# Two sets of transposes issued sooner, and one ScalarE relu, in a kernel bound by TensorE

## The chip, the cores, the metric

The kernel runs on one core of one Trainium2 chip. The metric is the device time of one execution in microseconds (us); lower is better. All executions quoted here are of the fast state, with a granted TensorE clock between 0.997 and 1.000. The engines are called PE (TensorE; PEld is its weight loads), VectorE (DVE in the profile), ScalarE (ACT), POOL (GpSimd) and SP (SyncE).

## The reference, cut to what matters

```python
# q, k, v: (8 batches, 8 heads, 576 rows, 64); w_in: 512 x 2048; w_out: 2048 x 512
kv  = einsum('bhsd,bhse->bhde', k, v)          # linear attention: no softmax
out = einsum('bhsd,bhde->bhse', q, kv)
x   = out / sqrt(mean(out*out, -1) + 1e-6) * g_norm    # per head; then (4608, 512)
h   = x @ w_in
g   = where(h > 0, h, exp(min(h, 0)) - 1)              # elu
y   = g @ w_out
```

Almost all of the work is in the two products of the last lines.

## The kernel before

The kernel works in nine stages: 512 rows of each of the eight batches, numbered 0 to 7, and a ninth stage for the rows left over. Stage T's expansion (`mm1`: eight products `i` of 256 hidden columns, 8 matmuls of 128x512 each) is interleaved with the contraction of stage T-1 (`mm2`) and with the attention of stage T+1 (the k-v products, the scores `out`, their norm), whose small matmuls stand between the large ones. **The program order on each engine is fixed by the order of the code**; nothing is reordered by a scheduler.

PSUM is the memory that TensorE writes its results to. Its eight banks are shared out like this: `at` is one tile of two banks, `mm1` two tiles of two banks each, and `mm2` two tiles of one bank each. Where all products use the `mm1` tiles, as in batch 2, product `i+2` takes the banks of product `i`, and PE cannot start it before the last reader of product `i` is done.

```python
def mm1(T, i, ..., relu=False, home="m1", between=()):
    ...                                   # 8 matmuls into both = [128, 2, 512] fp32 PSUM
    return elu(T, i, parts, relu, between)

def elu(T, i, parts, relu, between=()):
    e = mlpt.tile([P, 2, G], BF16, name="elu_e", tag="elu_e")
    for lo, hi, ps in parts:
        nc.scalar.activation(e[:, lo:hi, :], ps, AF.Exp)          # reads PSUM
    ...
    if relu:
        h = mlpt.tile([P, 2, G], BF16, name="elu_h", tag="elu_h", bufs=2)
        for lo, hi, ps in parts:
            nc.scalar.activation(h[:, lo:hi, :], ps, AF.Relu)     # last reader of PSUM
        parts = [(0, 2, h)]
    def rest():
        for lo, hi, h in parts:
            nc.vector.tensor_scalar(out=e..., in0=e..., 1.0, 1.0, op0=ALU.min, op1=ALU.subtract)
            nc.vector.tensor_tensor(out=gT[T]..., in0=e..., in1=h,
                                    op=ALU.add if relu else ALU.max)  # without relu: h is PSUM
    return rest
```

With `relu`, elu(h) is min(exp(h),1)-1 + relu(h), and ScalarE's relu is the last to read the PSUM banks. Without it, elu(h) is max(min(exp(h),1)-1, h), and VectorE's maximum, later in the chain, is the last to read them.

The normalised rows `xs` are turned into xT by PE transposes in batches 1 and 2 (later batches use DMA transposes), followed by a multiplication with g on the way out of PSUM:

```python
def x_u(u, eng):                          # batch 1: u = 0 on ScalarE, 1 on VectorE
    def turn(ps):
        for n in range(2):
            c = 2 * u + n
            for j in range(J):
                nc.tensor.transpose(xt[:, n, ...], st["xs"][:, j, c * P : c * P + P], ident)
        ...                               # xT[:, 2u:2u+2] = xt * g
```

`x_t` does the same for batch 2. The places at which these are called:

```python
    for j in range(J):                    # stage 0's contraction, f = 10, 11
        mm2(0, j, 10, 12)
        if j == 1:
            at["inv1"]()
            at["xu0"](scores[:, 0, :])
    at["mulu1"]()                         # VectorE: second half of xs
    ...
    for j in range(J):
        mm2(0, j, 12, 14)
    for j in range(J):
        mm2(0, j, 14, FC, hold=j > 1)     # FC = 16: two matmuls for each j
        if j == 2:
            at["xu1"](scores[:, 1, :])
    mm2_out(0, 2); mm2_out(0, 3)
    # ... [cut] then stage 1: mm1(1, 0) to mm1(1, 7), scores, norms of batch 2
    at["x0"]()
    mm2_quarter(1, 2, 0)                  # = mm2(1, 2, 0, 4): four matmuls
    at["x1"](ps_m1.tile([P, 2, G], FP32, name="xt_ps", tag="mm1")[:, 0, :])
    mm2_quarter(1, 2, 1)
    # ... [cut] stages 2 to 8:
        group(T, at, lead, second, {2: (1, 2, 4), B: ()}.get(T, (4, 5)))   # last: which i get the relu
```

## Time and profile before

| | before |
|---|---|
| time, median of 3 runs | 284.67 us (284.57 to 284.71) |
| span of the profiled run | 283.0 us |
| PE busy | 277.2 us, 98% |
| VectorE busy, ScalarE busy | 159.7 us, 153.5 us |

The page of the kernel before. The lines of groups give: line, engine, operation, output and input, their shapes, count, then busy us and mean ns of one, then the engine's idle time before them and what ended it.

```profile
span 283.0 us, 5186 instructions
PE 277.2 (98%) x2146; PEld 129.4 (46%) x2146; DVE 159.7 (56%) x231; ACT 153.5 (54%) x221; POOL 54.4 (19%) x96
...
PE 95%; DMA 2%; DVE 1%; issue 0%; SPq 0%; ACT 0%; DVEq 0%
...
L496 DVE TENSOR_TENSOR gT<-elu_e,h_ps 128x1024 bf16<-128x1024 bf16 (+1 forms) x52 | 61.4, 1180 | 5.8 <-DVE elu_e L488 0.5
...
L483 ACT ACTIVATE elu_h<-h_ps 128x1024 bf16<-128x1024 f32 (+1 forms) x19 | 18.5, 988 | 0.0
L496 DVE TENSOR_TENSOR gT<-elu_e,elu_h 128x1024 bf16<-128x1024 bf16 x19 | 13.2, 693 | 2.8 <-ACT elu_h L483 1.5
```

PE is 98% busy and 95% of the chain of work that ended last, so only time in which PE issues nothing can be won. "98% busy" hides what is left of it, because a matmul's shown duration (379 ns) is longer than the distance at which matmuls follow each other (216 ns): a stall of up to 160 ns leaves no idle time in the page. **The place to look is the distance between starts.** The timeline shows it, with a merged run of n matmuls lasting (n-1) x 216 + 379 ns when nothing is lost: 1.89 us for eight.

The timeline of the kernel before, at the three places that matter (start us, duration us, engine, line, operation, count; in brackets the idle time ahead and what ended it):

```profile
45.52 0.61 PE L413 MATMUL se_ps<-ident,xs 128*128 128x128 bf16 x8
45.97 0.59 PE L512 MATMUL o_ps<-w_out_sb,gT 128*128 128x512 bf16 x2
46.24 0.75 DVE L422 TENSOR_SCALAR xT<-se_ps,g_col 128x1024 bf16<-128x1024 bf16 x1 [1.67 <-PE se_ps L413]
46.40 2.10 PE L465 MATMUL at<-xT,w_in_sb 128*128 128x512 bf16 x8
...
68.03 1.28 DVE L229 TENSOR_TENSOR xs<-se_ps,ss 128x512 bf16<-128x512 f32 x2
70.14 0.61 PE L305 MATMUL xt_ps<-ident,xs 128*128 128x128 bf16 x8
70.58 1.03 PE L512 MATMUL o_ps<-w_out_sb,gT 128*128 128x512 bf16 x4
70.78 0.75 DVE L314 TENSOR_SCALAR xT<-xt_ps,g_col 128x1024 bf16<-128x1024 bf16 x1 [1.48 <-PE xt_ps L305]
71.59 0.60 PE L465 MATMUL h_ps<-xT,w_in_sb 128*128 128x512 bf16 x2
...
87.41 1.02 ACT L477 ACTIVATE elu_e<-h_ps 128x1024 bf16<-128x1024 f32 x1
89.49 1.22 DVE L496 TENSOR_TENSOR gT<-elu_e,h_ps 128x1024 bf16<-128x1024 bf16 x1
89.71 1.03 PE L512 MATMUL o_ps<-w_out_sb,gT 128*128 128x512 bf16 x4
90.77 1.02 PE L465 MATMUL h_ps<-xT,w_in_sb 128*128 128x512 bf16 x4
```

Three losses can be read here. At 46.40, eight matmuls of batch 1's first product take 2.10 us instead of 1.89: inside that run the third matmul, the first to need xT's second half, starts at 47.05, 214 ns late, when VectorE's multiplication (to 47.00) is done. At 71.59, batch 2's first product should have followed the four `o_ps` matmuls at 70.58 + 4 x 0.216 = 71.44; it is 148 ns late, released by the multiplication that ended at 71.54. At 90.77, batch 2's product 7 should have come at 89.71 + 0.864 = 90.57; it is 192 ns late, released by VectorE's maximum of product 5, which read PSUM until 90.71. Together that is 0.55 us. (Starts were read instruction by instruction; the two digits of the lines give the same within 10 ns.)

### The profile page before, as it was taken

To read this page: it belongs to the slowest core of one execution; us is meant where nothing else is said; L and a number is where in the kernel's file an instruction comes from. 1 tells how busy PE (TensorE), PEld (TensorE's weight loads), DVE (VectorE), ACT (ScalarE), POOL (GpSimd) and SP (SyncE) were. 2 spreads that over 40 slices of the span, in tenths; PEclk is the share of its full clock that TensorE was granted. 3 is DMA by queue.
4 is the path that set the end of the run, shared out by engine and by line. 5 is a ranking of instruction groups with operands and counts; after the bars stand their busy time and mean duration, and the time that the engine had idled before them with its cause. 6 is when DMAs were issued, how large, how long until landed. Compare 5 with 4: busy or idle time off the path is not lost.

```text
span 283.0 us, 5186 instructions
## 1 busy us (share of the span) xinstructions
PE 277.2 (98%) x2146; PEld 129.4 (46%) x2146; DVE 159.7 (56%) x231; ACT 153.5 (54%) x221; POOL 54.4 (19%) x96
## 2 busy tenths in 40 slices
PE   8999999999999999999999999999999999999994
PEld 3444544445444444444444444444444444444443
DVE  2359343877488646943694468445854585444400
ACT  2779546666486438533763378237923692333311
POOL 7834422151421331005200421012000000000000
PEclk9999999999999999999999999999999999999999
DMA  7999999696993695358935794355233123010122
GB/s 193 204 204 202 207 200 185 213 149 121 199 182 75 155 176 136 74 148 117 203 75 140 95 209 99 106 119 149 53 98 74 78 52 97 0 76 0 74 74 76
DMA packets 56523, 35.99 MB, mean 127 GB/s; under 512 B 32820, under 2 KB 54068, under 8 KB 56500
## 3 DMA queue, kind: packets, MB, share of 16 engines
q0 software_dynamic: 20752, 17.30, 40.3%
q1 hardware_dynamic: 35348, 17.83, 23.3%
q10 hardware_dynamic: 400, 0.52, 0.6%
q8 instruction: 17, 0.28, 0.4%
q14 instruction: 6, 0.05, 0.1%
HBM read 36.70 MB, written 9.44 MB: 163 GB/s over the span
## 4 chain that ended last, share of the span: by engine, by line
PE 95%; DMA 2%; DVE 1%; issue 0%; SPq 0%; ACT 0%; DVEq 0%
PE h_ps L465 42%; PE o_ps L512 39%; PE o_ps L917 5%; DMA st_q<-in_q_dram 2%; PE at L174 2%; PE bank L674 1%; PE at L465 1%; PE at L201 1%; PE h_ps L674 1%; PE bank L596 1%; PE bank L644 1%; PE se_ps L201 1%; PE kv_ps L174 0%; PE at L185 0%; PE se_ps L413 0%; DVE xT L422 0%
## 5 line engine op out<-in xcount | busy, mean ns | idle before, releaser
L465 PE MATMUL h_ps<-xT,w_in_sb 128*128 128x512 bf16 x536 | 125.7, 379 | 0.0
L512 PE MATMUL o_ps<-w_out_sb,gT 128*128 128x512 bf16 x512 | 120.5, 379 | 0.0
L477 ACT ACTIVATE elu_e<-h_ps 128x1024 bf16<-128x1024 f32 (+1 forms) x71 | 70.0, 995 | 81.3 <-PE h_ps L465 79.7
L465 PEld LDWEIGHTS <-w_in_sb 128*128 128x128 bf16 x552 | 52.4, 98 | 63.8 <-DVE xT L333 1.7
L512 PEld LDWEIGHTS <-gT 128*128 128x128 bf16 x512 | 49.4, 98 | 58.4
L488 DVE TENSOR_SCALAR elu_e<-elu_e 128x1024 bf16<-128x1024 bf16 (+1 forms) x75 | 32.3, 430 | 71.7 <-ACT elu_e L477 71.7
L496 DVE TENSOR_TENSOR gT<-elu_e,h_ps 128x1024 bf16<-128x1024 bf16 (+1 forms) x52 | 61.4, 1180 | 5.8 <-DVE elu_e L488 0.5
L525 ACT COPY o_sb<-o_ps 128x512 f32<-128x512 f32 x32 | 18.5, 586 | 15.7 <-PE o_ps L512 15.7
L218 DVE TENSOR_REDUCE ss<-sq 128x16 f32<-128x1024 bf16 x16 | 19.4, 1218 | 11.0 <-ACT sq L213 10.1
L150 POOL COPY q_bf<-q_pk 128x512 bf16<-128x512 bf16 x24 | 14.3, 628 | 22.3 <-DMA q_pk<-in_q_dram 22.3
L483 ACT ACTIVATE elu_h<-h_ps 128x1024 bf16<-128x1024 f32 (+1 forms) x19 | 18.5, 988 | 0.0
L496 DVE TENSOR_TENSOR gT<-elu_e,elu_h 128x1024 bf16<-128x1024 bf16 x19 | 13.2, 693 | 2.8 <-ACT elu_h L483 1.5
L917 PE MATMUL o_ps<-w_out_sb,gT 128*128 128x512 bf16 (+1 forms) x80 | 14.1, 337 | 0.0
L125 POOL COPY gate<-qT 1x1 bf16<-1x1 bf16 x6 | 1.1, 180 | 63.7 <-DMA qT<-q_bf 63.7
L104 POOL DMA_DIRECT2D q_pk<-in_q_dram x14 | 10.5, 756 | 2.9 <-issue 1.1
L229 DVE TENSOR_TENSOR xs<-at,ss 128x512 bf16<-128x512 f32 x16 | 10.2, 682 | 1.2 <-ACT ss L225 1.2
L917 PEld LDWEIGHTS <-gT 128*128 128x128 bf16 x80 | 7.8, 98 | 6.4 <-DVE gT L496 0.4
L213 ACT ACTIVATE sq<-at 128x1024 bf16<-128x1024 f32 x9 | 9.4, 1043 | 1.6 <-PE at L201 1.0
L118 POOL DMA_DIRECT2D k_pk<-in_k_dram x12 | 8.3, 693 | 4.7 <-DMA w_in_sb<-in_moe_w_in_dram 3.1
L118 POOL DMA_DIRECT2D v_pk<-in_v_dram x12 | 8.3, 694 | 4.4 <-DMA w_out_sb<-in_moe_w_out_dram 1.8
L596 PE MATMUL bank<-zeros 128*128 128x512 bf16 x20 | 7.4, 495 | 1.2 <-DVE zeros L573 1.2
L925 ACT COPY o_last<-o_ps 128x512 f32<-128x512 f32 (+1 forms) x5 | 2.5, 500 | 10.8 <-PE o_ps L917 10.8
(79 smaller groups left out, 139.2 us busy)
## 6 DMA issues: line engine op xcount, KB each, us to landing
out_dram<-o_sb SPq DMA_DIRECT2D x16, 512.0 KB, 3.0
q_pk<-in_q_dram POOLq DMA_DIRECT2D x14, 256.0 KB, 5.2
k_pk<-in_k_dram POOLq DMA_DIRECT2D x6, 576.0 KB, 8.0
v_pk<-in_v_dram POOLq DMA_DIRECT2D x6, 576.0 KB, 10.6
st_q<-in_q_dram SPq DMA_DIRECT2D x2, 512.0 KB, 4.8
w_in_sb<-in_moe_w_in_dram POOLq DMA_DIRECT2D x2, 512.0 KB, 9.0
w_out_sb<-in_moe_w_out_dram POOLq DMA_DIRECT2D x2, 512.0 KB, 15.7
w_out_sb<-in_moe_w_out_dram POOLq DMA_DIRECT2D x4, 256.0 KB, 11.8
```

What stands on the lines that cost most here:

```text
L104: nc.gpsimd.dma_start(out=t[:, 4 * s : 4 * s + 4].rearrange("p h j d -> p h (j d)"), in_=in_[:, s])
L118: nc.gpsimd.dma_start(out=raw[name, b].rearrange("p h j d -> p h (j d)")[:, hs], in_=in_[:, hs])
L150: eng.tensor_copy(out=out_, in_=in_)
L218: nc.vector.reduce_sum(out=ss, in_=sq.rearrange("p c (h e) -> p (c h) e", h=H), axis=AX.X)
L465: nc.tensor.matmul(h_ps[a][:, cs], lhsT=w_in_sb[:, c, f * P : f * P + P], rhs=x(c, cs), start=(c == 0), stop=(c == KC - 1),)
L477: nc.scalar.activation(e[:, lo:hi, :], ps, AF.Exp)
L483: nc.scalar.activation(h[:, lo:hi, :], ps, AF.Relu)
L488: nc.vector.tensor_scalar(out=e[:, lo:hi, :], in0=e[:, lo:hi, :], scalar1=1.0, scalar2=1.0, op0=ALU.min, op1=ALU.subtract,)
L496: nc.vector.tensor_tensor(out=gT[T][:, 2 * i + lo : 2 * i + hi, :], in0=e[:, lo:hi, :], in1=h, op=ALU.add if relu else ALU.max,)
L512: nc.tensor.matmul(o_ps[T, j], lhsT=gT[T][:, f, j * P : j * P + P], rhs=w_out_sb[:, f, :], start=(f == 0), stop=(f == FC - 1),)
L525: nc.scalar.copy(o_sb[T][:, j % 2, :], o_ps.pop((T, j)))
L917: nc.tensor.matmul(ps, lhsT=gT[B][:, f, j * P : j * P + P], rhs=w_out_sb[:, f, cols], start=(f == 0), stop=(f == FC - 1),)
```

## The change

The intent is to remove these three waits. Batch 1's second set of transposes moves ahead of four matmuls, batch 2's ahead of two, and product 5 of batch 2 gets the relu, so that ScalarE and not VectorE reads its banks last.

```diff
     for j in range(J):
         mm2(0, j, 14, FC, hold=j > 1)
-        if j == 2:
+        if j == 0:
             at["xu1"](scores[:, 1, :])
 ...
     at["x0"]()
-    mm2_quarter(1, 2, 0)
+    mm2(1, 2, 0, 2)
     at["x1"](ps_m1.tile([P, 2, G], FP32, name="xt_ps", tag="mm1")[:, 0, :])
-    mm2_quarter(1, 2, 1)
+    mm2(1, 2, 2, 8)
 ...
-        group(T, at, lead, second, {2: (1, 2, 4), B: ()}.get(T, (4, 5)))
+        group(T, at, lead, second, {2: (1, 2, 4, 5), B: ()}.get(T, (4, 5)))
```

## The prediction

> **What bounds the kernel.** TensorE: the page shows PE busy 98% of the 283.0 us span, and 95% of the chain that ended last. Successive 128x512 matmuls start 216 ns apart in the timeline, at a granted clock of 0.999; the Trainium skill ("TensorE: Matmul & The Clock Gate", Step-by-step) states about 216 ns, and the trace agrees. Only lost PE issue time can be won. Going through PE's timeline start by start after 18 us, I find beyond the usual pitch the switches to and from small matmuls (about 95 ns each, kept by the change) and three waits:
> - 47.05 us, third matmul of batch 1's first expansion product: 214 ns late. It waits for VectorE's g multiply of xT's second half (46.24 to 47.00), behind transposes issued at 45.52.
> - 71.59 us, batch 2's first product: 148 ns late, for the multiply of x1 (70.78 to 71.54) behind transposes at 70.14.
> - 90.77 us, batch 2's eighth product (i=7): 192 ns late. It takes the PSUM pair of product 5, whose last reader is VectorE's maximum straight from PSUM (89.49 to 90.71).
> Together 0.55 us. Batches 3 to 8 show no such wait over 50 ns.
>
> **What the change does.** Nothing is removed; one ScalarE relu is added.
> 1. Batch 1: eight transposes move ahead of four matmuls (4 x 216 ns = 0.86 us), to about 44.66. Their source is done at 44.57, its first half at 43.96, so they should not wait. VectorE, idle 1.67 us there, should multiply about 45.38 to 46.13, ahead of the first product. Gain 214 ns.
> 2. Batch 2: x1's transposes move ahead of two matmuls, to about 69.70; the source is done at 69.31. The multiply ends about 71.10 and the product can start at 71.44. Gain 148 ns, slack 0.3 us.
> 3. Product 5 of batch 2: ScalarE's relu takes about 1.0 us after its exp (87.41 to 88.43); ScalarE was idle 1.48 us there, so it fits. VectorE's last step goes from 1.22 us (fp32 from PSUM) to 0.69 us (bf16 in SBUF); the skill's "VectorE: DVE Perf Modes" (perf-mode tier table) gives tensor_tensor twice the rate on bf16 in SBUF, and this trace agrees (693 against 1220 ns). The pair comes free at the relu's end, about 89.4, over 1 us before PE wants it. Gain 192 ns.
>
> **On the critical path:** all three gains lie in PE's own stream, and what follows is PE work with slack behind it, so they add: 214 + 148 + 192 = 554 ns. The tail after the last matmul (about 4 us) just moves forward.
>
> **Predicted time:** 284.67 - 0.55 = 284.12 us, 0.2% faster; 80% range 283.90 to 284.45. Faster by over 2%: 0.005; within 2%: 0.99; slower by over 2%: 0.005. The three waits are nearly all there is to win.
>
> **What would show it.** The page: relu group x19 to x20, the bf16 gT add x19 to x20, the maximum from PSUM one fewer; span about 282.4. Timeline: each of the three late matmuls starts 216 ns after its predecessor.
>
> **What would make it wrong.** The transposes wait at their new places for VectorE's scaling (gains 1 or 2 halve, as a stall ahead of a transpose); the relu delays product 6's exp, whose PSUM pair becomes the next wait; more switch overhead at the new places; a DMA landing at a fixed time takes back what was won; or the scatter of 0.14 us blurs it.

## The result, and the profile after

| | before | after |
|---|---|---|
| time, median of 6 runs each | 284.69 us (284.54 to 284.73) | 284.19 us (284.08 to 284.47) |
| span of the profiled run | 283.0 us | 282.7 us |
| first transposes of batch 1's q to the last matmul, PE | 247.561 us | 247.005 us |

The ratio of the times is 0.9985, with a 95% interval of 0.9972 to 0.9998: a gain just clear of the noise. (A ratio is the mean time of one kernel's fast runs over that of the other's of the same rounds, so it is not quite the ratio of the medians quoted.)

The last row is a yardstick used below. The times of one kernel within a call scatter by 0.1 to 0.6 us, once by 0.8. Part of it arises before 31 us, where the first loads land: PE's first transposes of batch 1's q start between 31.05 and 31.59 us in the thirteen profiles. From their start to the start of the last matmul, PE's stream repeats far better: two profiles of the changed kernel gave 247.005 and 247.016 us. From the last matmul's start to the end of the span it is 4.09 to 4.11 us in all of them. This is also why the profiled span shrank by only 0.3 us: that run started this stretch at 31.59 us, against 31.30 before. (The other five runs of the changed kernel have spans of 282.3 to 282.4 us.)

The same lines of the page of the changed kernel:

```profile
span 282.7 us, 5187 instructions
PE 277.2 (98%) x2146; PEld 129.7 (46%) x2146; DVE 159.3 (56%) x231; ACT 154.5 (55%) x222; POOL 54.7 (19%) x96
...
PE 95%; DMA 2%; DVE 1%; SPq 0%; issue 0%; ACT 0%
...
L496 DVE TENSOR_TENSOR gT<-elu_e,h_ps 128x1024 bf16<-128x1024 bf16 (+1 forms) x51 | 60.1, 1179 | 5.7 <-DVE elu_e L488 0.5
...
L483 ACT ACTIVATE elu_h<-h_ps 128x1024 bf16<-128x1024 f32 (+1 forms) x20 | 19.5, 990 | 0.0
...
L496 DVE TENSOR_TENSOR gT<-elu_e,elu_h 128x1024 bf16<-128x1024 bf16 x20 | 13.8, 692 | 2.9 <-ACT elu_h L483 1.5
```

PE's busy time is 277.2 us in both: busy time does not show this gain. One maximum from PSUM became an addition from SBUF, and ScalarE has one relu more.

The timeline of the changed kernel at the same three places:

```profile
44.95 0.61 PE L413 MATMUL se_ps<-ident,xs 128*128 128x128 bf16 x8
...
45.40 1.46 PE L512 MATMUL o_ps<-w_out_sb,gT 128*128 128x512 bf16 x6
45.67 0.75 DVE L422 TENSOR_SCALAR xT<-se_ps,g_col 128x1024 bf16<-128x1024 bf16 x1 [0.81 <-PE se_ps L413]
...
46.69 1.89 PE L465 MATMUL at<-xT,w_in_sb 128*128 128x512 bf16 x8
...
68.10 1.28 DVE L229 TENSOR_TENSOR xs<-se_ps,ss 128x512 bf16<-128x512 f32 x2
...
69.78 0.61 PE L305 MATMUL xt_ps<-ident,xs 128*128 128x128 bf16 x8
...
70.22 1.46 PE L512 MATMUL o_ps<-w_out_sb,gT 128*128 128x512 bf16 x6
...
70.43 0.75 DVE L314 TENSOR_SCALAR xT<-xt_ps,g_col 128x1024 bf16<-128x1024 bf16 x1 [1.05 <-PE xt_ps L305]
...
71.52 0.81 PE L465 MATMUL h_ps<-xT,w_in_sb 128*128 128x512 bf16 x3
...
87.33 1.02 ACT L477 ACTIVATE elu_e<-h_ps 128x1024 bf16<-128x1024 f32 x1
...
88.23 1.03 ACT L483 ACTIVATE elu_h<-h_ps 128x1024 bf16<-128x1024 f32 x1
...
89.41 0.69 DVE L496 TENSOR_TENSOR gT<-elu_e,elu_h 128x1024 bf16<-128x1024 bf16 x1
...
89.62 1.03 PE L512 MATMUL o_ps<-w_out_sb,gT 128*128 128x512 bf16 x4
...
90.49 1.46 PE L465 MATMUL h_ps<-xT,w_in_sb 128*128 128x512 bf16 x6
```

The eight matmuls at 46.69 take 1.89 us, the undisturbed value; the multiplication ended at 46.42, before the product began. Batch 2's first product starts at 71.52, which is 70.22 + 6 x 0.216. Product 7 starts at 90.49, which is 89.62 + 4 x 0.216 within rounding; its banks were free from 89.26. All three gaps are gone; the other distances between PE's starts after 31 us, the switches of about 95 ns among them, are as they were.

### The profile page after: what moved, and what is told of

It reads as the page before. It is cut to its first block, busy times and chain, and to the rows that moved or that the text cites. A ratio compares the mean times of both kernels' runs of the same rounds, so it can differ in the third digit from the quotient of the medians.

```text
span 282.7 us, 5187 instructions
## 1 busy us (share of the span) xinstructions
PE 277.2 (98%) x2146; PEld 129.7 (46%) x2146; DVE 159.3 (56%) x231; ACT 154.5 (55%) x222; POOL 54.7 (19%) x96
## 4 chain that ended last, share of the span: by engine, by line
PE 95%; DMA 2%; DVE 1%; SPq 0%; issue 0%; ACT 0%
PE h_ps L465 41%; PE o_ps L512 39%; PE o_ps L917 5%; DMA st_q<-in_q_dram 2%; PE at L174 2%; PE bank L674 1%; PE at L465 1%; PE at L201 1%; PE h_ps L674 1%; PE bank L596 1%; PE bank L644 1%; PE se_ps L201 1%; PE kv_ps L174 0%; PE at L185 0%; PE se_ps L413 0%; PE bank L656 0%
## 5 line engine op out<-in xcount | busy, mean ns | idle before, releaser
L496 DVE TENSOR_TENSOR gT<-elu_e,h_ps 128x1024 bf16<-128x1024 bf16 (+1 forms) x51 | 60.1, 1179 | 5.7 <-DVE elu_e L488 0.5
L483 ACT ACTIVATE elu_h<-h_ps 128x1024 bf16<-128x1024 f32 (+1 forms) x20 | 19.5, 990 | 0.0
L496 DVE TENSOR_TENSOR gT<-elu_e,elu_h 128x1024 bf16<-128x1024 bf16 x20 | 13.8, 692 | 2.9 <-ACT elu_h L483 1.5
```

The lines of the kernel that those rows point to most:

```text
L496: nc.vector.tensor_tensor(out=gT[T][:, 2 * i + lo : 2 * i + hi, :], in0=e[:, lo:hi, :], in1=h, op=ALU.add if relu else ALU.max,)
```

## The experiments

Eleven kernels were run, all correct, all with five timed rounds. Theory A says that each part of the change removes exactly one PE wait, and that all PE work after it simply moves up. The rivals are named with each run. Kernels are compared only within the same rounds. The "stretch" is the yardstick above; it comes from one profile of each kernel. The interval of the timed ratio is about 0.13% wide to each side, 0.36 us, so the times alone cannot settle differences of 0.2 us; the gaps and the stretch can.

| run | what it is | median us | before | ratio (95% interval) | stretch, less before's |
|---|---|---|---|---|---|
| e1_batch1 | part 1 alone | 284.46 | 284.66 | 0.9991 (0.9979 to 1.0004) | -0.203 |
| e2_batch2 | part 2 alone | 284.45 | 284.66 | 0.9992 (0.9980 to 1.0005) | -0.150 |
| e3_relu5 | part 3 alone | 284.50 | 284.66 | 0.9992 (0.9980 to 1.0005) | -0.189 |
| e4_relu6 | relu on product 6 instead | 284.77 | 284.66 | 1.0002 (0.9988 to 1.0015) | +0.007 |
| e5_home | other banks for product 7, no relu | 284.37 | 284.56 | 0.9992 (0.9979 to 1.0004) | -0.185 |
| e6_half | part 1, half the move | 284.34 | 284.56 | 0.9990 (0.9977 to 1.0004) | -0.218 |
| e7_early | part 1, four matmuls further | 284.99 | 284.56 | 1.0015 (1.0002 to 1.0027) | +0.415 |
| e9_kvjoin_only | changed, a k-v product sooner | 285.31 | 284.56 | 1.0023 (1.0011 to 1.0036) | +0.654 |
| e10_after_again | the changed kernel again | 284.17 | 284.80 | 0.9975 (0.9961 to 0.9989) | -0.545 |
| e8_first_later | changed, first transposes later | 284.16 | 284.80 | 0.9977 (0.9965 to 0.9990) | -0.579 |
| e11_home_all | parts 1, 2 and e5's banks | 284.24 | 284.80 | 0.9976 (0.9964 to 0.9989) | -0.542 |

### Each part alone

Part 1 alone (`e1_batch1`):

```diff
-        if j == 2:
+        if j == 0:
             at["xu1"](scores[:, 1, :])
```

> Part 1 alone: only batch 1's second set of transposes moves four matmuls earlier. Theory A (each part removes exactly one PE wait and all that follows moves up): the 214 ns gap ahead of the third matmul of batch 1's first product goes, the gaps of 148 ns and 192 ns in batch 2 stay, time 0.21 us below the kernel before. Theory B (the gain is one effect of an earlier batch 1, and the batch 2 waits close or open with it): the batch 2 gaps change by more than 30 ns, time not 0.21 us below.

```profile
46.43 1.89 PE L465 MATMUL at<-xT,w_in_sb 128*128 128x512 bf16 x8
```

Measured: the first gap is gone; the two in batch 2 stay at 146 and 192 ns. The stretch is 0.203 us shorter, the median 0.20 us lower.

Part 2 alone (`e2_batch2`):

```diff
-    mm2_quarter(1, 2, 0)
+    mm2(1, 2, 0, 2)
     at["x1"](...)
-    mm2_quarter(1, 2, 1)
+    mm2(1, 2, 2, 8)
```

> Part 2 alone: only x1's transposes of batch 2 move two matmuls earlier. Theory A: the 148 ns gap ahead of batch 2's first product goes, the gaps of 214 ns (batch 1) and 192 ns (product 7) stay, time 0.15 us below the kernel before. Theory B (what is won there is given back at product 7, which waits for VectorE): the gap at product 7 grows from 192 to about 340 ns and the time does not change.

```profile
70.01 1.46 PE L512 MATMUL o_ps<-w_out_sb,gT 128*128 128x512 bf16 x6
71.30 0.81 PE L465 MATMUL h_ps<-xT,w_in_sb 128*128 128x512 bf16 x3
```

Measured: the gap ahead of batch 2's first product is gone, the others stay at 214 and 194 ns. So product 7's wait does not take the gain back: the VectorE chain that releases it starts from PE's own products and moves up with them. The stretch is 0.150 us shorter; the median is 0.21 lower, more than expected but within the scatter.

Part 3 alone (`e3_relu5`):

```diff
-        group(T, at, lead, second, {2: (1, 2, 4), B: ()}.get(T, (4, 5)))
+        group(T, at, lead, second, {2: (1, 2, 4, 5), B: ()}.get(T, (4, 5)))
```

> Part 3 alone: product 5 of batch 2 gets the ScalarE relu. Theory A (its PSUM pair comes free earlier): the 192 ns gap ahead of product 7 goes, the 214 and 148 ns gaps stay, time 0.19 us below the kernel before. Rival (ScalarE's extra 1.0 us delays product 6's exp or the output copies): a new PE gap after 91 us, gain under 0.1 us.

Measured: the gap ahead of product 7 is gone, the others stay at 214 and 147 ns, and no new gap over 50 ns appears after 91 us. The stretch is 0.189 us shorter, the median 0.16 lower.

The three together make 0.203 + 0.150 + 0.189 = 0.542 us; the change as a whole shows 0.556 and 0.545. **The parts add.** None is eaten by another, and none hides another.

### What in part 3 counts: the banks or the VectorE time?

The relu does two things: it frees the banks sooner and it takes 0.5 us off VectorE. The control `e4_relu6` keeps the second without the first:

```diff
-        group(T, at, lead, second, {2: (1, 2, 4), B: ()}.get(T, (4, 5)))
+        group(T, at, lead, second, {2: (1, 2, 4, 6), B: ()}.get(T, (4, 5)))
```

> Control for part 3: the relu goes to product 6 of batch 2 instead of 5. VectorE saves the same 0.5 us, but product 7's PSUM pair, last read for product 5, comes free no sooner. Theory A (the pair's release is what counts): the 192 ns gap ahead of product 7 stays, time within 0.06 us of the kernel before. Rival (VectorE's shorter work in batch 2 is what counts): gain of about 0.19 us as in part 3 alone.

The timeline of this kernel around product 7:

```profile
89.53 1.22 DVE L496 TENSOR_TENSOR gT<-elu_e,h_ps 128x1024 bf16<-128x1024 bf16 x1
...
89.74 1.03 PE L512 MATMUL o_ps<-w_out_sb,gT 128*128 128x512 bf16 x4
...
90.80 0.81 PE L465 MATMUL h_ps<-xT,w_in_sb 128*128 128x512 bf16 x3
...
90.86 1.02 ACT L483 ACTIVATE elu_h<-h_ps 128x1024 bf16<-128x1024 f32 x1
```

Product 7 still starts 90.80 - 90.60 = 0.20 us late, behind the maximum that ends at 90.75. The relu at 90.86 belongs to product 6 and comes too late to matter; so does VectorE's saving, whose shorter step starts only at 91.91. This control shows that a saving elsewhere in the batch gives nothing, but not that one ahead of product 7 would. The stretch is unchanged (+0.007 us).

The converse, `e5_home`, frees product 7 of its wait without any relu, by giving it the two banks that the scores left at about 88 us:

```diff
-                rest = mm1(T, i, relu=i in relu, between=early)
+                rest = mm1(T, i, relu=i in relu, between=early, home="at" if i == 7 else "m1")
```

> No relu is added; product 7 of batch 2 writes another PSUM pair instead, the one that the scores left at about 88 us. ScalarE and VectorE do the same work as in the kernel before. Theory A (the pair's release is what counts): the 192 ns gap ahead of product 7 goes, time 0.19 us below the kernel before, as with the relu. Rival (the gain comes from VectorE's shorter or ScalarE's earlier work): the gap stays or moves to the next product, gain under 0.06 us.

```profile
89.49 1.22 DVE L496 TENSOR_TENSOR gT<-elu_e,h_ps 128x1024 bf16<-128x1024 bf16 x1
89.51 1.03 PE L512 MATMUL o_ps<-w_out_sb,gT 128*128 128x512 bf16 x3
...
90.38 0.81 PE L465 MATMUL at<-xT,w_in_sb 128*128 128x512 bf16 x3
```

These lines of its timeline show VectorE's maximum lasting as long as before, to 90.71, while product 7 starts at 90.38, which is 89.51 + 4 x 0.216 (one of the four `o_ps` records is missing from this trace). The stretch is 0.185 us shorter, as with the relu. This run settles it, since its VectorE does all the work of the kernel before: the release of the banks is enough, and VectorE's saving is not needed. `e11_home_all` below finds nothing beyond it either.

### How far to move the transposes

Half of part 1's move (`e6_half`):

```diff
-        if j == 2:
+        if j == 1:
             at["xu1"](scores[:, 1, :])
```

> Batch 1 alone with half the move: the transposes go two matmuls earlier instead of four. Theory A (only the wait itself can be won; the multiply would end about 46.57 us and the third matmul wants to start at 46.84): the whole 214 ns gap goes, time 0.21 us below the kernel before, as with the full move. Rival (the gain grows with how much sooner the transposes go): about half, 0.1 us, with a gap of some 100 ns left.

```profile
45.42 1.03 PE L512 MATMUL o_ps<-w_out_sb,gT 128*128 128x512 bf16 x4
45.69 0.75 DVE L422 TENSOR_SCALAR xT<-se_ps,g_col 128x1024 bf16<-128x1024 bf16 x1 [1.24 <-PE se_ps L413]
...
46.28 1.03 PE L465 MATMUL at<-xT,w_in_sb 128*128 128x512 bf16 x4
```

The multiplication ends at 46.44; the third matmul is due at 46.28 + 0.43 = 46.71 and there is no gap in this run of matmuls. The whole gain is there (-0.218 us): a wait can be removed only once, and what goes beyond its length is slack.

Four matmuls further than the change, which makes eight from the old place (`e7_early`). The expectation below says two further; that is a slip, as the edit passes two matmuls of `f` = 12, 13 as well as six of the last loop:

```diff
     for j in range(J):
         mm2(0, j, 12, 14)
+        if j == 2:
+            at["xu1"](scores[:, 1, :])
     for j in range(J):
         mm2(0, j, 14, FC, hold=j > 1)
-        if j == 2:
-            at["xu1"](scores[:, 1, :])
```

> Batch 1 alone, the transposes two matmuls earlier still than in the change, which asks for their source (done at 44.57 us in the kernel before) before it is written. Theory A: the 214 ns gap goes, but a new one of 150 to 300 ns stands ahead of or within these transposes, and the time is within 0.1 us of the kernel before. Rival (sooner is better): time at least 0.2 us below the kernel before.

```profile
42.68 1.03 PE L512 MATMUL o_ps<-w_out_sb,gT 128*128 128x512 bf16 x4
42.90 1.10 ACT L420 ACTIVATE xT<-se_ps,g_col 128x1024 bf16<-128x1024 bf16 x1
43.03 1.29 DVE L391 TENSOR_TENSOR xs<-at,ss 128x512 bf16<-128x512 f32 x2 [0.62 <-ACT ss L225]
...
43.77 0.10 PEld L413 LDWEIGHTS <-xs 128*128 128x128 bf16 x1 [0.56 <-DVE xs L391]
44.05 0.72 PE L413 MATMUL se_ps<-ident,xs 128*128 128x128 bf16 x8 [0.34 <-ACT xT L420]
...
44.61 2.32 PE L512 MATMUL o_ps<-w_out_sb,gT 128*128 128x512 bf16 x10
```

This is a loss, larger than expected: 0.43 us above the kernel before by the medians, 0.415 by the stretch. The line at 44.61 shows the true length of the move: ten `o_ps` matmuls follow the transposes, against six in the changed kernel and two before. The transposes are due at 42.68 + 0.86 = 43.54 and start 508 ns late, at 44.05. The trace puts that wait down to ScalarE's reading of the first set of transposes (until 44.00), which sits in the other bank of the same two-bank PSUM tile; I had not reckoned with it. Inside them another 105 ns go to VectorE's scaling of the second half of xs, which ends at 44.32. The bill agrees: 508 + 105 - 214 = 399 ns.

Of these two waits VectorE's is the one that sets the loss. The fifth transpose needs the second half of xs and starts at 44.38, just behind the scaling. Without ScalarE's wait the first four could have started sooner (their half of xs was done at 43.72), but not the fifth. So the scaling, which the expectation named, accounts for all of the 508 + 105 = 613 ns; two separate PSUM tiles, not tried, should win nothing here. At two matmuls further, the place that the expectation meant, the same scaling would leave an estimated 613 - 2 x 216 = 181 ns, within the expected 150 to 300 ns; that place was not run. Of the places tried for these transposes, counted in matmuls from the old one, two and four matmuls earlier win the whole wait, and eight lose more than there was to win.

### Going on: two further ideas

The largest loss left in PE's stream is the switch between large and small matmuls, about 95 ns each way, 18 times in and 18 times out after 31 us: an estimated 36 x 95 ns = 3.4 us, six times what the change wins. `e9_kvjoin_only` puts the second k-v product of batch 1 right behind the first score product, to save two switches:

```diff
         if j == 2:
             at["seu0"](scores)
             at["sq0"]()
+            at["kvu1"]()
             at["sum0"]()
     for j in range(J):
         mm2(0, j, 8, 10)
         if j == 1:
-            at["kvu1"]()
             at["inv0"]()
             at["mulu0"]()
```

> The changed kernel with one thing more: the second k-v product of batch 1 goes right behind the first score product, so that PE has one stretch of small matmuls there instead of two (two switches of about 95 ns saved). Theory A (PE's issue time is all that can be won, but a wait for VectorE's scaling, 43 ns today ahead of batch 1's first transposes, stands right behind): PE arrives there 0.2 us sooner while the scaling ends at most 0.1 us sooner, so that wait grows to 150 to 250 ns; 0 to 0.1 us below the changed kernel, 0.5 to 0.65 us below the kernel before. Rival (a saved switch is always won in full): 0.19 us below the changed kernel, 0.74 below the kernel before.

```profile
36.19 0.41 PE L373 MATMUL se_ps<-kv_sb,qT 64*128 64x64 bf16 x16
...
37.88 0.48 PE L174 MATMUL at<-v_pk,k_pk 64*64 64x64 bf16 x36 [1.28 <-DMA v_pk<-in_v_dram]
```

Neither expectation held. The product waits until 37.88 for the second half of batch 1's v, whose DMA lands at 37.74 us. In the kernel before that landing is at 38.06 us and the product starts at 38.56: there the order of the code left just 0.5 us for it, and nothing in the profile of waits says so, because a wait that is met costs nothing. The gap is 1.446 us; less the two switches (93 + 98 ns) and the 43 ns wait behind it, which disappears, that is 1.212 us, and the stretch is 248.215 - 247.005 = 1.210 us longer than the changed kernel's.

The changed kernel ran again beside two variants.

> The changed kernel unaltered, to stand beside the next two on one chip. Theory A: 0.50 to 0.55 us below the kernel before; PE's three gaps gone.

Measured: 284.17 us against 284.80, 0.63 us lower, a little more than expected; one of the nine runs of the kernel before took 285.51 us. The stretch, -0.545 us, is the steadier number.

`e8_first_later` moves batch 1's first transposes out of the last VectorE wait in this part, 43 ns at 41.48 us:

```diff
         if j == 1:
             at["inv1"]()
+        if j == 2:
             at["xu0"](scores[:, 0, :])
```

> The changed kernel, with batch 1's first set of transposes moved two matmuls later, out of the 43 ns that PE still waits there for VectorE's scaling. ScalarE takes up their result only after the second half's inverse roots, so it should start no later. Theory A (every PE wait removed is won, however small): that 43 ns gap goes and the last PE matmul starts 0.04 us sooner relative to the first product; time 0.04 us below the changed kernel, which the scatter of 0.1 us may hide. Rival (the later transposes make the first product of batch 1 wait): a new gap of over 50 ns ahead of it.

Measured: the 43 ns gap is gone and no other appears; the stretch is 247.016 - 246.982 = 0.034 us shorter than the changed kernel's. The time, 284.16 against 284.17 us, does not resolve it. It is the shortest stretch of all, but no faster kernel by the clock.

`e11_home_all` has parts 1 and 2 with e5's banks in place of the relu.

```diff
-        group(T, at, lead, second, {2: (1, 2, 4, 5), B: ()}.get(T, (4, 5)))
+        group(T, at, lead, second, {2: (1, 2, 4), B: ()}.get(T, (4, 5)))
 # and, in group, for T == 2:
-                rest = mm1(T, i, relu=i in relu, between=early)
+                rest = mm1(T, i, relu=i in relu, between=early, home="at" if i == 7 else "m1")
```

> Parts 1 and 2 of the change, with the other PSUM pair for product 7 of batch 2 in place of the relu of part 3. Theory A: no PE gap over 50 ns in batches 1 and 2, time within 0.06 us of the changed kernel, ScalarE 1.0 us less busy and VectorE 0.5 us busier than there. Rival (part 3 gives something beyond the pair's release): over 0.1 us slower than the changed kernel.

Measured: no gap over 50 ns in batches 1 and 2; the stretch differs from the changed kernel's by 0.003 us (247.019 against 247.016). The median, 284.24, is 0.07 us above it, just past the expected 0.06 and within the scatter. ScalarE is busy 153.6 us against 154.5, VectorE 159.3 against 158.7 in `e10_after_again`. (The first profile of the changed kernel has 159.3 for VectorE too, so its expected 0.5 us is not resolved.) The relu of part 3 gives nothing beyond the release of the banks.

## Why the prediction was right

- **The bound, and the size of what can be won.** The prediction took its 0.55 us from three distances between matmul starts. The change removed those three and nothing else: 0.556 us of PE's stretch, 0.50 us by the medians (284.69 to 284.19), against a predicted 284.12.
- **Part 1** was to have the transposes at about 44.66, the multiplication from 45.38 to 46.13. The profile has 44.95 and 45.67 to 46.42, all later by the 0.29 us with which this run left its first stage late. Gain predicted 214 ns, shown alone 203.
- **Part 2** was to have x1's transposes at 69.70; the profile has 69.78, which is 69.70 plus 0.29 of the late start less part 1's 0.21. Predicted 148 ns, shown alone 150.
- **Part 3** was to free the banks at about 89.4; they came free at 89.26. VectorE's step went from 1.22 to 0.69 us as predicted; the size was that of the trace. The perf-mode tier table of the Trainium skill ("VectorE: DVE Perf Modes") gives the direction, twice the rate for bf16 in SBUF, but the trace's factor is 1.8 and not 2, and data type, memory and operation all changed at once here, so no run shows which of them counts. Predicted 192 ns, shown alone 189. The controls show that this VectorE saving had no part in the gain.
- **Adding them** was right: 542 ns from the parts alone, 556 and 545 together.
- **What was off, slightly.** The span was predicted at about 282.4 us; the profiled run has 282.7, for the late first stage, and the other five have 282.3 to 282.4. The prediction's fear that the transposes might wait for VectorE's scaling was sound: with four matmuls more (`e7_early`) it costs 613 ns. ScalarE's reading of the first set, which the prediction did not name, holds the first 508 of them too, but ends sooner.

## What to carry to other kernels

When an engine is at 98%, list the distances between starts of its successive instructions and compare them with the undisturbed pitch; the few that are longer are what can be won without taking work or switches off that engine. Here the released work followed on the same engine, and the three gains added. Move a producer only as far as removes the wait: before its place stand other waits, met so far, that no view of waits lists (0.5 us of slack on a landing here). When a PSUM bank is what is waited for, ask who reads it last. Here another reader and another bank were worth the same (0.189 and 0.185 us), and VectorE's own busy time was worth nothing.

## What the Trainium skill lacked or had wrong

- "TensorE: Matmul & The Clock Gate", Back-to-back issue gap: it says that a stream of weight load and matmul pairs sustains about 131 ns for each 512-column matmul, and that 216 ns over-counts. In every run here such a stream keeps to 216 ns (eight in 1.89 us, of which the last shows 379 ns); the same page's 216 ns in Step-by-step is right for this kernel.
- The same page, Part 3, The mechanism: it lists that a weight load overlaps with matmuls in flight only when the row group differs. Here 128x128 weight loads of 98 ns, all on the same full set of rows, leave no trace in the 216 ns pitch of the matmuls (the background weight buffer that the section names earlier would fit this).
- The same page has no figure for a switch between 128-row matmuls and the 64-row ones of the attention; "TensorEngine Tiling (Array Packing)", Key Properties, says that a change of tiling mode drains the engine, also without a figure. In the nine profiles without missing records, 92 to 97 ns of PE's stream are lost on the way in; on the way out 118 to 128 ns pass from the start of the last small matmul to that of the first large one.
- The same page, Part 4, PE-mode transpose: about 275 ns in a kernel's context. Here a 128x128 bf16 transpose shows 219 ns, and eight in a row start 56 ns apart (0.61 us for eight), so in a row they cost a fifth of that figure each.
- "Perfetto Trace Analysis", Identifying the Most-Contended Engine: it warns that matmul busy time says little about the distance to the roofline, and offers MFU (the share of peak matmul work) and the busy share of the weight loads instead. The busy shares do not show this gain: PE busy is 277.2 us before and after, PEld 129.4 and 129.7. The gaps between slices, which the page says to look for under Optimization Strategy, show little of it: the stalls of 214, 192 and 148 ns leave 51, 29 and 0 ns between PE's slices. What shows them in full is the distance between matmul starts, which the page does not propose.
